# Moving a clip, a store and half a weight transfer in a Mamba2 block with a gated feed-forward

## The chip, the cores and the metric

The kernel runs on one core of one Trainium2 chip. A core has TensorE (PE in the profile, with its weight loads as PEld), VectorE (DVE), ScalarE (ACT), GpSimd (POOL) and SyncE (SP), which here only issues transfers. The metric is the time of one execution on the device, in microseconds, lower is better. Three executions of the kernel before took 349.08, 349.23 and 349.53 us; the median is 349.23 us.

## The reference

Two stages, one behind the other. The first is a Mamba2 state-space block over 4 batches, 8 heads, 768 positions, head dimension 32 and state dimension 16, in chunks of 32. The second is a feed-forward layer on the 3072 x 256 result: 2048 hidden columns with a quick GELU, and back to 256.

```python
log_a = np.log(np.clip(a, 1e-06, 1.0))
for c in range(nc):
    cum = np.cumsum(la, axis=-1)
    L = np.exp(cum[..., :, None] - cum[..., None, :]) * causal
    y_intra = einsum(CB * L, xc)
    y_inter = einsum(Cc, state) * np.exp(cum)
    y[:, :, sl] = y_intra + y_inter
    state = decay_full * state + sum(Bx)
...
h = x @ w_in
g = h * (1.0 / (1.0 + np.exp(-1.702 * h)))
return g @ w_out
```

The weights `w_in` and `w_out` come as float64, the decays `a` as float32.

## The kernel before

The 3072 tokens are worked through in six groups (g) of 512. The state-space block of a group is done in two pairs (p) of 256 tokens, so pair 2 and pair 3 belong to group 1. While the feed-forward of one group runs on TensorE, the state-space work of the next is put between its matmuls. The order of every engine's instructions is the order of the program: `in_order` ties each instruction to the one before it on its engine. So an instruction that waits holds up all that stands behind it on that engine.

**The weights.** Both weight matrices arrive as pairs of 32-bit words and are turned into float32 on the chip, in ten pieces. Pieces 0 to 3 are two blocks of `w_in` each (128 hidden columns a block), pieces 4 and 5 four blocks each, pieces 6 to 9 four blocks of `w_out` each. For piece i:
- `fetch(i)` (line 163) issues two transfers on SyncE (line 180), one per half k of the 256 input rows. Pieces 0 and 1 share one buffer. With `held`, an engine first writes one element of the buffer (line 171), so that a transfer which overwrites this element has to wait for that engine to get there.
- `fields(i)` (lines 192 and 195) takes exponent and mantissa apart on VectorE, into `p` (power) and `m`.
- `clamp(i)` (lines 203 and 204) limits the exponent on ScalarE, in two instructions.
- `rounded(i)` (line 208) adds the low word on VectorE.
- `join(i, parts)` (lines 222 and 228) puts sign, exponent and mantissa together on VectorE and writes `w_in` or `w_out`; with parts = 2 in two rounds, so that the first blocks are ready sooner. It needs `clamp(i)`. After join(1) follows fetch(6), after join(5) fetch(9).
- `narrow(i)` (line 235) is rounded(i), fields(i + 1) and join(i), with the join ahead of the fields for pieces 4 and 5, there in two parts.

**The first group.** At the start SyncE issues B, piece 0 and the four transfers of x for pairs 0 and 1. Then comes `fetch(1, held=nc.gpsimd)`: GpSimd writes element 0 of the buffer after its first `since_start`, and SyncE's transfers of pieces 1 to 5 and of `az` (the decays) follow. After that TensorE computes the hidden blocks f = 0 to 15 of group 0 (`hidden`, matmuls L895, activations L898). What is put behind each of them stands in `in_hidden[0]`: narrow(2) after block 1, narrow(3) after 2, narrow(4) after 4, narrow(5) after 8, narrow(6) after 11, narrow(7) after 14, and clamp(3) to clamp(8) after blocks 1, 2, 7, 11, 14 and 15. Work that is put behind the same block runs in the order in which it was added.

**The decays.** `az` holds `a` for the six chunks of 128 of each row. `clip(t, name)` (lines 356 to 361) limits its values, copies the first column of every half chunk into `starts` and sets these columns to zero in `az`. `store_a` (line 1225) clips all of `az` and has SyncE store it into `scratch` in DRAM (two transfers, line 1228); it runs after block 5, ahead of fetch(7), fetch(8) and the load of pair 3. `pick_a` (line 369) makes X from chunks 4 and 5 of `az` on ScalarE after block 8. `fan_all` after block 9 spreads X over the partitions with TensorE (ab, line 415, and the rows of lines 504 and 533) and scans it on VectorE (`decay_heads`, line 453); `since_fanned` (lines 543 to 546) follows. These serve pair 2. For pair 3, `spread` (line 259) reads `scratch` back into the tile `a`, and `spread_rows(1)` (line 268) reads `af`; both are issued after block 9.

**The projection of group 0** (`project_all`, matmuls L992 into o) has its own list, `in_project[0]`: the transposes of pair 2, rounded(8), fields(9) and join(8) at step 0; at step 2 `decay(3)` (scan at line 405 over `a`, then Be, line 464), `clip_rows(1)` and `decay_rows(1)` (lines 483 to 496, over `af`) and the transposes of pair 3, whose last part is `since_start(3)` (CsT, line 670). At step 9 TensorE takes `score` (cb, line 685) and `gain` (A, line 716).

```python
at(in_hidden[0], 5, store_a, lambda: fetch(7), lambda: fetch(8),
   lambda: load(PG + 1))
at(in_hidden[0], 8, lambda: pick_a(PG))
at(in_hidden[0], 9, lambda: fan_all(PG))
at(in_hidden[0], 9, since_fanned)
```

Of the kernel before, what the change touches and what calls it, by code (L numbers as in the profile page):

```python
# [8 lines left out]
FP32 = mybir.dt.float32  # L9
# [7 lines left out]
P = 128  # L17
# [18 lines left out]
def kernel(  # L36
# [31 lines left out]
    nc = tc.nc  # L68
# [6 lines left out]
    BH = NB * NH  # L75
# [7 lines left out]
    CG = TG // P  # L83
    NP = T // (2 * P)
    PG = CG // 2
# [9 lines left out]
    const = ctx.enter_context(tc.tile_pool(name="const", bufs=1))  # L95
# [10 lines left out]
    az = ffn.tile([P, 4 * TG // 2], FP32, tag="mg", name="az", bufs=3)[:, :NC * P].rearrange(  # L106
        "p (c s) -> p c s", c=NC)
# [8 lines left out]
    def load_blocks(p, queues=(nc.sync, nc.sync)):  # L116

        g, n = divmod(p, PG)
        b, c = divmod(2 * p, NC)
        for queue, name, src in zip(queues, "CB", (C, B)):  # L120
            if n == 0:
                blocks[name, g] = raw.tile([P, 2, PG * P], FP32, tag="z", name=f"z{name}{g}", bufs=2)
            for r in range(R):
                queue.dma_start(
                    out=blocks[name, g][32 * r:32 * r + 32, :, n * P:(n + 1) * P],
                    in_=src[b, Q * r:Q * r + Q, c * P:(c + 2) * P].rearrange(
                        "q (i f) n -> i q (f n)", i=32))
# [10 lines left out]
    def load(p, parts=None):  # L138
        if parts is None:
            parts = "bcx" if p < 2 * PG else "bx"  # L140
            if p >= 2 * PG:
                load_blocks(p)
        for part in parts:
            dst, src, e = {"b": (rb, B, N), "c": (rc, C, N), "x": (rx, x, D)}[part]
            dst[p] = raw.tile([P, 2, NH, e], FP32, tag=part, name=f"{part}{p}",
                              bufs=2 if part == "c" else 3)
            for k in range(2):
                b, c = divmod(2 * p + k, NC)
                sl = slice(c * P, (c + 1) * P)
                nc.sync.dma_start(out=dst[p][:, k], in_=src[b, :, sl, :].rearrange("h s d -> s h d"))  # L150
# [9 lines left out]
    def words(name):  # L160
        return wide.tile([P, 2 * PN], U32, tag="bits", name=name, bufs=BUFS)

    def fetch(i, held=False):
        name, f, n = PIECES[i]
        if n == 2 and f % 4:
            t = pieces.pop(i - 1)[:, 2 * n * DM:]
        else:
            t = pieces[i] = words(f"bits{i}")
            t = t[:, :2 * n * DM]
        if held:  # L170
            held.memset(t[:, :1], 0)
        if name == "in":
            src = moe_w_in[:, 2 * f * P:2 * (f + n) * P].rearrange("(k p) e -> p k e", p=P)
            dst, src = (v.rearrange(s, h=n, e=2 * P) for v, s in (
                (t, "p (h k e) -> k p h e"), (src, "p k (h e) -> k p h e")))
        else:
            src = moe_w_out[f * P:(f + n) * P, :].rearrange("(f p) (h e) -> h p f e", p=P, h=2)
            dst = t.rearrange("p (h f e) -> h p f e", h=2, f=n)
        for k in range(2):
            nc.sync.dma_start(out=dst[k], in_=src[k])  # L180
        t = t.rearrange("p (e w) -> p e w", w=2)
        bits[i] = t[:, :, 0], t[:, :, 1]
# [5 lines left out]
    def fields(i):  # L188
        hi, cols = bits[i][1], slice(0, PIECES[i][2] * DM)
        mantissa[i] = wide.tile([P, PN], U32, tag="m", name=f"m{i}")[:, cols]  # L190
        power[i] = wide.tile([P, PN], U32, tag="p2", name=f"p2{i}")[:, cols]
        nc.vector.tensor_scalar(out=power[i], in0=hi, scalar1=0x7FF00000, scalar2=None,
                                op0=ALU.bitwise_and)

        nc.vector.tensor_scalar(out=mantissa[i], in0=hi, scalar1=0x000FFFFF,
                                scalar2=0x00100000, op0=ALU.bitwise_and, op1=ALU.bitwise_or)
# [9 lines left out]
    def rounded(i):  # L206

        nc.vector.scalar_tensor_tensor(out=mantissa[i].bitcast(FP32), in0=bits[i][0],
                                       scalar=2.0 ** -32, in1=mantissa[i],
                                       op0=ALU.mult, op1=ALU.add)  # L210
# [4 lines left out]
    def join(i, parts=1):  # L215

        name, f, n = PIECES[i]
        n //= parts
        low, m, p2 = bits.pop(i)[1], mantissa.pop(i), power.pop(i)
        for k in range(parts):  # L220
            cols, fs = slice(k * n * DM, (k + 1) * n * DM), slice(f + k * n, f + (k + 1) * n)
            nc.vector.scalar_tensor_tensor(out=p2[:, cols], in0=low[:, cols], scalar=0x80000000,  # L222
                                           in1=p2[:, cols], op0=ALU.bitwise_and, op1=ALU.bitwise_or)
            if name == "in":
                dst, h = w_in[:, fs].rearrange("p f k e -> p (f k e)").unsqueeze(1), 1
            else:
                dst, h = w_out[:, :, fs].rearrange("p c f e -> p c (f e)"), 2
            nc.vector.scalar_tensor_tensor(  # L228
                out=dst, in0=m[:, cols].bitcast(FP32).rearrange("p (h e) -> p h e", h=h),
                scalar=2.0 ** -20, in1=p2[:, cols].bitcast(FP32).rearrange("p (h e) -> p h e", h=h),  # L230
                op0=ALU.mult, op1=ALU.mult)
        for n in NEXT.get(i, ()):
            fetch(n)

    def narrow(i):
        rounded(i)
        if i in (4, 5):
            join(i, 2)
        if i + 1 < len(PIECES):
            fields(i + 1)  # L240
        if i not in (4, 5):
            join(i)


    scratch = dram.tile([NC, 2, NB * NH, H], FP32, name="scratch")
# [106 lines left out]
    starts, fans, flat = {}, {}, {}  # L352

    def clip(t, name):

        nc.vector.tensor_scalar(out=t, in0=t, scalar1=1e-6, scalar2=1.0,
                                op0=ALU.max, op1=ALU.min)
        starts[name] = const.tile([P, t.shape[1], 2], FP32, name=f"starts{name}")
        first = t.rearrange(by_chunk, s=2)[:, :, :, 0]
        nc.vector.tensor_copy(starts[name], first)  # L360
        nc.vector.memset(first, 0.0)

    def pick_a(p):

        b, c = divmod(2 * p, NC)
        X = ffn.tile([P, 2, DM], FP32, tag="ob", name=f"X{p}")
        X = fans[p] = X.rearrange("p k (q i) -> p k q i", q=Q)
        for q in range(Q):
            nc.scalar.activation(X[:, :, q], az[:, c:c + 2], AF.Copy, scale=pick[:, b, q:q + 1])
# [13 lines left out]
    for i, n, head in ((0, 1, PG), (1, 2, PG), (0, 0, 1)):  # L383
        t = whose[32 * i:32 * i + 32, n:n + 1]
# [116 lines left out]
    def fan_rows(t, c0, c1, o):  # L501

        o = o[:, :(c1 - c0) * P]
        nc.tensor.matmul(out=o, lhsT=whose[:32, 0].rearrange("p h n -> p (h n)"),
                         rhs=t[:32, c0:c1].rearrange("p c s -> p (c s)"), start=True,
                         stop=True, tile_position=(0, 0), skip_group_check=True)
        return o
# [21 lines left out]
    def fan_since():  # L529
        o = bank("rows4")  # L530
        t = fanned["rows"] = fan_rows(az, CG, NC, o)
        f = fanned["starts"] = o[:, 2 * P:2 * P + 2 * (NC - CG)]
        nc.tensor.matmul(out=f, lhsT=whose[:32, 0].rearrange("p h n -> p (h n)"),
                         rhs=starts[1][:32, CG:].rearrange("p c s -> p (c s)"), start=True, stop=True,
                         tile_position=(0, 0), skip_group_check=True)

    fanned = {}
# [46 lines left out]
    def bank(name):  # L584
        return ps.tile([P, 4 * P], FP32, tag="ff", name=name)
# [634 lines left out]
    def at(places, i, *work):  # L1220
        places.setdefault(i, []).extend(work)

    in_hidden = [{} for _ in range(NG)]
    in_project = [{} for _ in range(NG)]
    def store_a():
        clip(az, 1)
        for i, side in enumerate(SIDES):
            nc.sync.dma_start(out=scratch[:, i].rearrange("c r i -> r c i"), in_=az[:32, :, side])

    at(in_hidden[0], 5, store_a, lambda: fetch(7), lambda: fetch(8),  # L1230
       lambda: load(PG + 1))
    at(in_hidden[0], 8, lambda: pick_a(PG))
    at(in_hidden[0], 9, lambda: fan_all(PG))
    at(in_hidden[0], 9, since_fanned)
    for i, k, c in ((2, 1, 1), (3, 2, 2), (4, 4, 7), (5, 8, 11), (6, 11, 14), (7, 14, 15)):
        at(in_hidden[0], k, lambda i=i: narrow(i))
        at(in_hidden[0], c, lambda i=i: clamp(i + 1))
    at(in_hidden[0], 9, lambda: spread(PG + 1), lambda: spread_rows(1))
    n, p = 2 * PG, 3 * PG
# [105 lines left out]
    for g in range(2, NG):  # L1345
        n, p = (g + 1) * PG, (g + 2) * PG
# [103 lines left out]
```

## Time and profile before

| | |
|---|---|
| median of three executions | 349.23 us (349.08 to 349.53) |
| the profiled execution, whole | 350.67 us |
| its span | 348.80 us |
| TensorE busy | 341.6 us (98%) |
| VectorE busy | 254.6 us (73%) |
| ScalarE busy | 155.0 us (44%) |
| GpSimd busy | 13.1 us (4%) |
| bytes moved | 25.92 MB |

A row of a timeline has the start in us from the beginning of the span, the duration in us, the engine (with q for its queue or sequencer, as in SPq), the line of the kernel, the operation, output<-inputs by the names of the tiles without their numbers, the shape, and how many instructions are merged in the row. In brackets stands how long the engine was idle before it, and what ended that. A float32 matmul appears as two records. A row of SyncE gives the time that issuing took; when the bytes land is told by the semaphore that the transfer raises.

### The profile page before, as it was taken

What the parts mean: (1) busy time and instruction counts of PE and PEld (TensorE: products, weight loads), DVE (VectorE), ACT (ScalarE), POOL (GpSimd) and SP (SyncE); (2) the same over time, 40 slices, a digit from 0 to 9 for tenths busy, and PEclk for the clock granted to TensorE, in tenths of its full rate; (3) what the DMA queues carried; (4) which work ended last, traced back from release to release, by engine and by line L of the source; (5) the groups of instructions that cost most, each with busy time, mean ns of one, the idle gap of its engine ahead of it and who ended that gap; (6) DMA issues with size and microseconds to landing.
All of it is one profiled execution on the core that took longest, in us unless ns stands there. A gap on an engine that the chain in (4) does not pass through costs nothing.

```text
span 348.8 us, 8124 instructions
## 1 busy us (share of the span) xinstructions
PE 341.6 (98%) x3380; PEld 268.9 (77%) x3380; DVE 254.6 (73%) x481; ACT 155.0 (44%) x352; POOL 13.1 (4%) x42
## 2 busy tenths in 40 slices
PE   8989999999999999999999999999999999999996
PEld 6634444445688888888888888888888888899996
DVE  5889997999878999667997467788465654465463
ACT  4797585205453322654432554332564331554320
POOL 8300000100000100000000000000000000000000
PEclk9999999999999999999999999999999999999999
DMA  6599889624627200415704027400000300000301
GB/s 158 134 300 213 189 181 245 113 54 105 113 49 131 66 0 2 75 57 124 123 18 63 0 59 130 73 1 2 0 4 3 55 7 0 0 2 0 62 0 61
DMA packets 89980, 25.92 MB, mean 74 GB/s; under 512 B 73432, under 2 KB 87128, under 8 KB 89944
## 3 DMA queue, kind: packets, MB, share of 16 engines
q1 hardware_dynamic: 89112, 24.88, 33.5%
q10 hardware_dynamic: 832, 0.52, 0.5%
q8 instruction: 26, 0.43, 0.5%
q14 instruction: 10, 0.08, 0.1%
HBM read 22.15 MB, written 3.24 MB: 73 GB/s over the span
## 4 chain that ended last, share of the span: by engine, by line
PE 90%; DMA 3%; DVE 2%; SPq 1%; ACT 1%; issue 1%; ACTq 1%; POOL 0%; DVEq 0%
PE acc L1055 28%; PE X L950 19%; PE Y L960 14%; PE o L992 8%; PE acc L1062 7%; PE h L895 5%; DMA bits<-in_moe_w_in_dram 3%; PE y L839 2%; PE cb L685 2%; PE y L825 1%; SPq L180 1%; PE A L716 1%; PE ab L557 1%; DMA zC<-in_C_dram 1%; DVE p L222 1%
## 5 line engine op out<-in xcount | busy, mean ns | idle before, releaser
L955 ACT ACTIVATE ac<-X 128x256 f32<-128x256 f32 x76 | 29.1, 383 | 81.5 <-PE X L950 80.7
L1082 DVE TENSOR_TENSOR gT<-Y,ac 128x512 f32<-128x512 f32 x38 | 26.2, 689 | 40.1 <-PE Y L960 32.5
L1055 PE MATMUL acc<-mg,mw 128*128 128x256 f32 x192 | 54.5, 379 | 0.0
L927 ACT ACTIVATE gT<-gT 128x512 f32<-128x512 f32 (+1 forms) x76 | 38.9, 518 | 29.0 <-DVE gT L1082 28.5
L950 PE MATMUL X<-my,mi 128*128 128x256 f32 x152 | 45.1, 380 | 0.0
L1055 PEld LDWEIGHTS acc<-mg,mw 128*128 128x128 f32 x192 | 36.5, 190 | 5.0
L895 PE MATMUL h<-yT,w_in 128*128 128x512 f32 x80 | 35.6, 598 | 1.1 <-DVE w_in L228 0.6
L1082 DVE TENSOR_TENSOR gT<-Y,b 128x256 f32<-128x256 f32 x38 | 15.9, 419 | 28.5 <-PE Y L960 28.5
L1055 PE MATMUL acc<-gT,w_out 128*128 128x256 f32 x128 | 35.5, 379 | 0.0
L950 PEld LDWEIGHTS X<-my,mi 128*128 128x128 f32 x152 | 28.0, 190 | 3.9 <-ACT ac L955 0.2
L895 PEld LDWEIGHTS h<-yT,w_in 128*128 128x128 f32 x80 | 14.7, 190 | 19.7 <-issue 15.9
L992 PE MATMUL o<-gT,w_out 128*128 128x512 f32 x64 | 28.3, 595 | 0.0
L918 DVE TENSOR_TENSOR mg<-gT 128x512 f32<-128x512 f32 x40 | 27.2, 681 | 0.0
L1055 PEld LDWEIGHTS acc<-gT,w_out 128*128 128x128 f32 x128 | 24.2, 190 | 3.4 <-ACT yT L873 0.2
L955 ACT ACTIVATE b<-X 128x256 f32<-128x256 f32 x38 | 14.6, 383 | 21.2 <-PE X L950 20.7
L950 PE MATMUL X<-yT,w_in 128*128 128x256 f32 x76 | 23.2, 389 | 0.0
L960 PE MATMUL Y<-yT,w_in 128*128 128x256 f32 x76 | 22.7, 381 | 0.0
L960 PE MATMUL Y<-my,mi 128*128 128x256 f32 x76 | 22.7, 380 | 0.0
L960 PE MATMUL Y<-yT,mi 128*128 128x256 f32 x76 | 22.5, 379 | 0.0
L950 PE MATMUL X<-my,w_in 128*128 128x256 f32 x76 | 22.5, 379 | 0.0
L992 PEld LDWEIGHTS o<-gT,w_out 128*128 128x128 f32 x64 | 11.8, 190 | 13.6 <-issue 13.4
L405 DVE TENSOR_TENSOR_SCAN L<-a,idents 128x1024 f32<-128x1024 f32 x9 | 20.5, 2277 | 0.2 <-DMA a<-scratch 0.2
(159 smaller groups left out, 546.9 us busy)
## 6 DMA issues: line engine op xcount, KB each, us to landing
a<-scratch SPq DMA_DIRECT2D x18, 256.0 KB, 4.8
bits<-in_moe_w_out_dram SPq DMA_DIRECT2D x8, 512.0 KB, 6.6
x<-in_x_dram SPq DMA_DIRECT2D x24, 128.0 KB, 3.1
out_dram<-ob SPq DMA_DIRECT2D x40, 64.0 KB, 1.9
bits<-in_moe_w_in_dram SPq DMA_DIRECT2D x8, 256.0 KB, 4.4
bits<-in_moe_w_in_dram SPq DMA_DIRECT2D x4, 512.0 KB, 11.9
b<-in_B_dram SPq DMA_DIRECT2D x20, 64.0 KB, 2.6
af<-in_a_dram SPq DMA_DIRECT2D x3, 384.0 KB
```

The costliest lines, as they stand in the source:

```text
L405: nc.vector.tensor_tensor_scan(out=L, data0=ra[p].rearrange("p k e -> p (k e)"), data1=idents.rearrange("p h i -> p (h i)"), initial=0.0, ...
L685: nc.tensor.matmul(out=s["cb"][side, r, k].rearrange("p (q i) -> p q i", q=Q), lhsT=BT[rows, k, side], rhs=CT[rows, k, :, side], start=Tru ...
L895: nc.tensor.matmul(out=h, lhsT=w_in[:, f, k], rhs=yT[g][:, k], start=(k == 0), stop=(k == NK - 1), skip_group_check=True)
L918: nc.vector.tensor_tensor(out=t[:, 0:2], in0=B[:, :, 1], in1=B[:, 0], op=ALU.subtract)
L927: nc.scalar.activation(o, i, AF.Silu, scale=GELU_SCALE)
L950: nc.tensor.matmul(out=s["X"], lhsT=lhsT, rhs=rhs, start=i == "1", stop=i == "4", skip_group_check=True)
L955: nc.scalar.activation(copy, s["X"], AF.Copy)
L960: nc.tensor.matmul(out=o, lhsT=lhsT, rhs=rhs, start=s.pop("new", False), stop=i != "5", skip_group_check=True)
L992: nc.tensor.matmul(out=o[c], lhsT=w_out[:, c, f], rhs=gT[g, f // 2][:, f % 2], start=(f == 0), stop=(f == NF - 1), skip_group_check=True)
L1055: nc.tensor.matmul(out=acc[g][0][i][:, cols], lhsT=w, rhs=h[:, cols], start=(j == 0 and k == 0 and (i, 0) in begins), stop=(j == NF // 2 - ...
L1062: nc.tensor.matmul(out=o[k] if type(o) is list else o[:, cols], lhsT=h[:, cols], rhs=w, start=(j == 0 and (i, k) in begins), stop=(j == NF ...
L1082: nc.vector.tensor_tensor(out=o, in0=v, in1=w, op=ALU.add)
```

## The change

- The element that GpSimd writes before piece 1 is no longer element 0 but element 256. The transfer of half k = 0 writes elements 0 to 255 and 512 to 767 of the piece, half k = 1 writes 256 to 511 and 768 to 1023. So only the second half overwrites the element.
- narrow(2) has its join ahead of fields(3). narrow(3) has its join in two parts, still behind fields(4).
- The clip of `az` is split. Chunks 4 and 5 (all 128 partitions) are clipped inside narrow(4), between join(4) and fields(5), and leave the starts that `fan_since` uses. Chunks 0 to 3 (32 partitions) are clipped in `store_a`, without starts.
- `store_a` stands after block 9, behind since_fanned and ahead of the spread of pair 3, not after block 5.
- `pick_a` stands after block 7, ahead of clamp(5), not after block 8.

```diff
         if held:
-            held.memset(t[:, :1], 0)
+            held.memset(t[:, 2 * P:2 * P + 1], 0)
...
     def narrow(i):
         rounded(i)
-        if i in (4, 5):
-            join(i, 2)
+        if i in (2, 4, 5):
+            join(i, 1 if i == 2 else 2)
+        if i == 4:
+            clip(az[:, CG:], 1)
         if i + 1 < len(PIECES):
             fields(i + 1)
-        if i not in (4, 5):
-            join(i)
+        if i not in (2, 4, 5):
+            join(i, 2 if i == 3 else 1)
...
-        starts[name] = const.tile([P, t.shape[1], 2], FP32, name=f"starts{name}")
+        if name:
+            starts[name] = const.tile([P, t.shape[1], 2], FP32, name=f"starts{name}")
         first = t.rearrange(by_chunk, s=2)[:, :, :, 0]
-        nc.vector.tensor_copy(starts[name], first)
+        if name:
+            nc.vector.tensor_copy(starts[name], first)
...
-                         rhs=starts[1][:32, CG:].rearrange("p c s -> p (c s)"), start=True, stop=True,
+                         rhs=starts[1][:32].rearrange("p c s -> p (c s)"), start=True, stop=True,
...
     def store_a():
-        clip(az, 1)
+        clip(az[:BH, :CG], 0)
...
-    at(in_hidden[0], 5, store_a, lambda: fetch(7), lambda: fetch(8),
-       lambda: load(PG + 1))
-    at(in_hidden[0], 8, lambda: pick_a(PG))
+    at(in_hidden[0], 5, lambda: fetch(7), lambda: fetch(8), lambda: load(PG + 1))
+    at(in_hidden[0], 7, lambda: pick_a(PG))
     at(in_hidden[0], 9, lambda: fan_all(PG))
-    at(in_hidden[0], 9, since_fanned)
+    at(in_hidden[0], 9, since_fanned, store_a)
```

## The prediction

> **What bounds the kernel now.** I read the page first, then the chain of waits up to 120 us, then the timeline of each engine from 11 to 69 us, and last when single transfers land.
>
> ```profile
> PE 341.6 (98%) x3380; PEld 268.9 (77%) x3380; DVE 254.6 (73%) x481; ACT 155.0 (44%) x352; POOL 13.1 (4%) x42
> ```
>
> TensorE is busy 98% of 348.8 us, so only holes in its work can be won, and any new hole is paid in full. The change touches work before 70 us, where the TensorE timeline has these holes:
>
> ```profile
> 18.38 7.18 PE L895 MATMUL h<-yT,w_in 128*128 128x512 f32 x16 [0.47 <-ACT yT L858]
> ...
> 26.18 10.57 PE L895 MATMUL h<-yT,w_in 128*128 128x512 f32 x24 [0.63 <-DVE w_in L228]
> ...
> 37.59 0.69 PE L415 MATMUL ab<-X,ones 32*64 32x256 f32 x16 [0.84 <-ACT X L369]
> ...
> 38.95 10.57 PE L895 MATMUL h<-yT,w_in 128*128 128x512 f32 x24
> ...
> 67.53 0.78 PE L716 MATMUL A<-x,Be 64*32 64x64 f32 x54 [0.31 <-DVE CsT L670]
> ```
>
> One block of the hidden layer is four records of 0.43, 1.72 us. Block 4 waits 0.63 for its weights; the 24 records after it take 10.57 where 24 x 0.43 = 10.3, so another 0.25 is lost (block 6); ab waits 0.84. The last line matters most: A waits for VectorE's CsT, so VectorE's chain at 67.5, and not TensorE, sets the rest. VectorE's own timeline:
>
> ```profile
> 22.50 0.69 DVE L208 SCALAR_TENSOR_TENSOR m<-bits,m 128x512 f32<-128x512 uint32 x1
> ...
> 23.94 0.43 DVE L192 TENSOR_SCALAR p<-bits 128x512 uint32<-128x512 uint32 x1 [0.75 <-DMA bits<-in_moe_w_in_dram]
> ...
> 26.87 0.69 DVE L192 TENSOR_SCALAR p<-bits 128x1024 uint32<-128x1024 uint32 x1 [0.24 <-DMA bits<-in_moe_w_in_dram]
> ...
> 34.41 0.55 DVE L356 TENSOR_SCALAR az<-az 128x768 f32<-128x768 f32 x1
> ...
> 36.35 0.70 DVE L222 SCALAR_TENSOR_TENSOR p<-bits,p 128x512 uint32<-128x512 uint32 x1
> ...
> 40.23 2.43 DVE L453 TENSOR_TENSOR_SCAN L<-ab,idents 128x256 f32<-128x256 f32 x4
> ...
> 57.72 0.69 DVE L192 TENSOR_SCALAR p<-bits 128x1024 uint32<-128x1024 uint32 x1 [1.77 <-DMA bits<-in_moe_w_out_dram]
> ...
> 61.32 2.28 DVE L405 TENSOR_TENSOR_SCAN L<-a,idents 128x1024 f32<-128x1024 f32 x1
> ...
> 64.05 0.56 DVE L483 TENSOR_SCALAR af<-af 128x768 f32<-128x768 f32 x1
> ...
> 67.04 0.42 DVE L670 TENSOR_TENSOR CsT<-tp,since 128x256 f32<-128x256 f32 x1
> ```
>
> It is full from 24 to 45 us, waits 1.77 for the last w_out piece, then runs without a break through decay(3) (61.32) to CsT. Its inputs a and af come through SyncE:
>
> ```profile
> 37.37 1.09 SPq L1228 DMA_DIRECT2D scratch<-az  x2
> 38.51 2.12 SPq L180 DMA_DIRECT2D bits<-in_moe_w_out_dram  x4
> ...
> 50.14 1.08 SPq L180 DMA_DIRECT2D bits<-in_moe_w_out_dram  x2
> 51.31 1.30 SPq L259 DMA_DIRECT2D a<-scratch  x2
> 52.66 0.72 SPq L268 DMA_DIRECT2D af<-in_a_dram  x1
> ```
>
> The store to scratch goes out 14 us before scratch is read back, and by its semaphore it has landed at 40.1. The pair a lands at 59.28 and 60.60, only 0.7 before decay(3) uses it, and af at about 63.2, 0.85 before 64.05.
>
> **The change part by part.**
>
> *First half of blocks 2 and 3 unheld.* SyncE issues the last x until 9.06, then waits 3.6 us for GpSimd's memset at 12.63. Now one transfer of 256 KB goes out at 9.1, behind x, and uses the stretch from 11 to 14 us in which the DMA engines are under 10% busy. All ten transfers behind the memset move up one issue (0.47 us). At 385 GB/s, the rate of 23 to 26 us, 256 KB less ahead is 0.68 us; at the 200 GB/s of 14 to 17 us, 1.3. Ends 0.5 and 1.3; I take 0.7, since the pieces land in the fast stretch. Pieces 3 and 4 landed at 23.85 and 26.75, now about 23.1 and 26.0. Cost: the last x landed at 11.92, and A (12.02) uses it in its last quarter, at 12.5; an x with 512 KB behind it (issued 49.21) took 3.85 us against 3.44, which gives 12.3: nothing, at most 0.4.
>
> *join(2) before fields(3).* It now waits for ScalarE's clamp(2), which ends at 23.64 by the row of before, not for a DMA: 23.68 to 25.09 instead of 24.62 to 26.03. TensorE's block 4 starts at 25.56, when block 3 ends: 0.63 gone. VectorE waits 0.45 instead of 0.75, and fields(4) starts at 26.48 instead of 26.87.
>
> *join(3) in halves.* Four instructions of 128x256 at the 0.40 spacing of 16.22 to 17.81 are 1.6 instead of 1.4: 0.2 more on VectorE, but block 6 has its weights at 28.6 and needs them at 29.0: 0.25 gone.
>
> *The clip split.* Narrow(4) ends at 33.13 (33.21 before). The half for chunks 4 and 5 is 128x256: 0.42 for 512 columns and 0.55 for 768 put it at 0.29, and the row of 0.50 for 128x256 at 4.28 is the upper end; with starts and memset 0.55 (0.45 to 0.8). It now stands before fields(5), where it stood behind it: fields(5) at 33.7 (33.21). X needs the clip: 33.8 to 34.7 on ScalarE, ahead of clamp(5), which takes 2.33 and ends at 37.0 (36.26). ab then never waits: TensorE gets there at 35.9 instead of 37.59, 1.7 us won. But join(5) waits for clamp(5): 37.05 instead of 36.35, and everything behind it on VectorE is 0.7 late. The other half (32x512, 0.42 by the row of that width, and memset) comes after since_fanned: another 0.5, less the 0.33 that fields(7) waited for a piece that now lands earlier. join(6) ends at 50.0 instead of 49.12. TensorE, finished with block 15 at 47.6, waits for these w_out blocks: o starts at 50.25 instead of 49.79. So the 1.7 won is given back at 50 us, and 0.45 more. At A this is 0.45 late against a wait of 0.3 to 0.48: nothing to speak of.
>
> *The store behind since_fanned.* On SyncE its two issues (1.14 us) no longer stand ahead of fetch(7), fetch(8) and the loads of pair 3; with the 0.7 above, fetch(9) goes out 1.1 to 1.9 earlier (48.6) and lands at 56.1 (55.5 to 56.4) instead of 57.59. VectorE is ready for it at 56.7, so decay(3) could start at 60.3, 1.0 earlier. But the store is now issued right behind fetch(9), at about 49.8, with 1 MB ahead of it in its queue (before, it landed 0.4 behind the x ahead of it), and the read of scratch right behind the store. The trace of before never shows this wait. I have SyncE hold the read until the store has landed. The Trainium skill, "DMA: Bandwidth & Descriptors", section "Two DMAs through the same engine are not ordered", says a dependent DMA must be issued only after the first one's completion semaphore; no run here shows what happens without it.
>
> The store lands at 56.1 (55.5 to 56.8). From there the pair a: unqueued pairs landed 5.3 us (76.51) and 5.5 (103.71) after the first issue; the pair with af behind it, as here, 6.55:
>
> ```profile
> 152.06 1.24 SPq L259 DMA_DIRECT2D a<-scratch  x2
> 153.40 0.64 SPq L268 DMA_DIRECT2D af<-in_a_dram  x1
> ```
>
> Nearest is the last; I take 6.0: a at 62.1 (60.8 to 63.3). af, 8.8 after the first issue there, is at 64.9, in time for a clip_rows at 64.9. decay(3) starts at 62.1 instead of 61.32, so CsT and A are 0.8 later. SyncE's later loads slip about 1 us, and the nearest user (79.33; landed by 74.1) has 5 to spare.
>
> **Sum.** TensorE: -0.63 -0.25 -0.84, given back at o, +0.45, absorbed at A; then +0.8 at A by the wait for a. The profiled execution, 350.67 (span 348.80 and 1.87 around it; 1.44 above the median), becomes 351.5; the median of 349.23 becomes 350.0.
>
> **Rivals.**
> 1. *The round trip is hidden.* If a lands by 61.3, A is bound by TensorE: -0.05, up to 0.2 either way; 349.2. For it: fetch(9) may go out 2 us earlier and two of three pairs took 5.4. Against it: the store has 1 MB ahead, and the pair that had af behind it took 6.55. The Trainium skill, "DMA: Bandwidth & Descriptors", section "Anatomy of one DMA", fits a fixed 2.0 us and 436 GB/s for transfers that GpSimd issues, by which (an estimate) the pair would land 3.2 us after its issue and be hidden; the trace, of SyncE's transfers, has 5.3 to 6.55.
> 2. *Faster: VectorE's chain is shorter than I count.* If ScalarE and the clip cost so little that join(6) ends by 49.0 and a lands by 60.5, A moves up with decay(3), at most 1.0: 348.4. For it: VectorE loses three DMA waits (0.75, 0.24, 0.33). Against: clamp(5) cannot start before power(5), which stands behind the clip. It decides when both are 0.7 earlier than my count.
> 3. *The half transfer is not free*, or stays held after all, because the memset lies between its columns: the queue gains nothing, a lands 0.7 later still, or A at 12 us slips 0.4: 350.8.
>
> **Numbers.** Forecast (a binds, 0.4 to 1.5 late) 0.47; rival 1 0.30; rival 2 0.15; rival 3 0.08. The bound for no change is 0.2%, 0.7 us, about what a measurement of this kernel can tell. Of the forecast's 0.47 some 0.06 lie under 0.7; rival 3 gives 0.07 to slower. So faster 0.17, same 0.35, slower 0.48. The range goes from rival 2's middle, 348.5, to 351.2, the pair at its slowest (+1.5 to +2); the forecast's own is 349.6 to 350.8.
>
> **What would show it.** Right: block 4 and ab without a hole; o's first matmul waiting for DVE w_out near 50; SyncE waiting for scratch; decay(3) waiting for DMA a near 62; A later than 68. Wrong: decay(3) starts without a DMA wait, or o waits for nothing at 48.2.

## The result and the profile after

The changed kernel took 353.52 us (median of six, 352.22 to 354.81), the kernel before, beside it, 349.15 us (median of six, 348.80 to 349.56). The ratio is 1.0124 with a 95% interval of 1.0101 to 1.0147: slower by 1.2%. The forecast was 350.0 and its range ended at 351.2, so the direction was right and the size was wrong. (The ratios leave out executions at a much lower clock, two of the kernel before at 503 us and one of e8 at 587 us, and are not always the quotient of the two medians.)

The profiled execution of the changed kernel took 352.22 us, the fastest of its six; its span is 350.2. The first part of its page:

```profile
PE 341.7 (98%) x3380; PEld 268.6 (77%) x3380; DVE 255.0 (73%) x485; ACT 155.0 (44%) x352; POOL 13.2 (4%) x42
```

TensorE does the same work; the time went into holes. Rows of its timeline from 11 to 69 us:

```profile
16.54 0.76 PE L843 MATMUL y<-L,x 64*32 64x64 f32 x53 [1.43 <-issue]
...
19.26 17.43 PE L899 MATMUL h<-yT,w_in 128*128 128x512 f32 x40 [0.47 <-ACT yT L862]
36.63 0.69 PE L419 MATMUL ab<-X,ones 32*64 32x256 f32 x16
...
50.59 3.67 PE L996 MATMUL o<-gT,w_out 128*128 128x512 f32 x8 [1.60 <-DVE w_out L228]
...
67.78 0.79 PE L720 MATMUL A<-x,Be 64*32 64x64 f32 x56
```

The hidden layer runs 40 records in 17.43 without a hole, and ab no longer waits: both as forecast. Then o waits 1.60 for VectorE's w_out, as forecast too, and A comes at 67.78 without a wait, which was not forecast. VectorE's timeline of the same kernel shows why o is late:

```profile
21.15 0.69 DVE L222 SCALAR_TENSOR_TENSOR p<-bits,p 128x512 uint32<-128x512 uint32 x1 [1.30 <-ACT p L204]
...
24.45 0.69 DVE L222 SCALAR_TENSOR_TENSOR p<-bits,p 128x512 uint32<-128x512 uint32 x1 [0.48 <-ACT p L204]
...
37.65 0.69 DVE L222 SCALAR_TENSOR_TENSOR p<-bits,p 128x512 uint32<-128x512 uint32 x1 [0.71 <-ACT p L204]
...
60.65 2.28 DVE L409 TENSOR_TENSOR_SCAN L<-a,idents 128x1024 f32<-128x1024 f32 x1
62.97 0.49 DVE L468 TENSOR_TENSOR Be<-b,L 128x128 f32<-128x128 f32 x2
63.74 0.56 DVE L487 TENSOR_SCALAR af<-af 128x768 f32<-128x768 f32 x1 [0.28 <-DMA af<-in_a_dram]
...
66.74 0.42 DVE L674 TENSOR_TENSOR CsT<-tp,since 128x256 f32<-128x256 f32 x1
```

VectorE waits for clamp(1) (1.30), clamp(2) (0.48) and clamp(5) (0.71), and for af by a little. decay(3) at 60.65 does not wait for a, which the prediction had named as a sign of being wrong. CsT is done at 67.16, 0.6 before A, so in this execution A is held by the late o and not by VectorE. SyncE's row of issues and its waits, in two answers:

```profile
46.42 1.08 SPq L180 DMA_DIRECT2D bits<-in_moe_w_out_dram  x2
47.59 1.24 SPq L1232 DMA_DIRECT2D scratch<-az  x2
53.01 1.35 SPq L261 DMA_DIRECT2D a<-scratch  x2
```

```profile
SPq L261 <- DMA scratch<-az: 4.1, 1, 4.1
```

SyncE stands 4.1 us at the read of scratch (total, times, longest). By the semaphores fetch(9) landed at 52.75, the store at 52.96 and 53.17, and the pair a at 58.99.

**The kernel before, a second time.** The prediction read an execution of 350.67 us. Among the other 81 timed executions of the kernel before (348.44 to 351.22), taken beside the result and the experiments, one was slower than that. So the same kernel was profiled once more, as e5: 349.15 us, span 347.2. Its TensorE timeline:

```profile
15.57 0.76 PE L839 MATMUL y<-L,x 64*32 64x64 f32 x53 [0.60 <-issue]
...
18.30 17.43 PE L895 MATMUL h<-yT,w_in 128*128 128x512 f32 x40 [0.47 <-ACT yT L858]
36.48 0.69 PE L415 MATMUL ab<-X,ones 32*64 32x256 f32 x16 [0.75 <-ACT X L369]
...
48.69 3.60 PE L992 MATMUL o<-gT,w_out 128*128 128x512 f32 x8
...
65.81 0.79 PE L716 MATMUL A<-x,Be 64*32 64x64 f32 x56
```

and its VectorE timeline:

```profile
20.19 0.69 DVE L222 SCALAR_TENSOR_TENSOR p<-bits,p 128x512 uint32<-128x512 uint32 x1 [0.45 <-ACT p L204]
...
58.38 2.29 DVE L405 TENSOR_TENSOR_SCAN L<-a,idents 128x1024 f32<-128x1024 f32 x1
...
64.10 0.42 DVE L670 TENSOR_TENSOR CsT<-tp,since 128x256 f32<-128x256 f32 x1
```

The hole at block 4, that at block 6 and the wait at A are not there. VectorE waits for no piece of weights, decay(3) starts 2.9 earlier than in the profile that the prediction read, and CsT is done at 64.5, 1.3 before A. Against this execution the changed kernel's TensorE is 0.96 late at y, 0.14 at ab (the 0.75 there is won), 1.90 at o, 1.97 at A, 2.5 at 113 us and 2.94 at 121 us, where X waits 0.35 for ac. That is the 3.0 between the spans.

The 0.96 at y is a part of this that no experiment ties to the change. It does not stay on TensorE: ScalarE's yT and the clamp(1) behind it come 0.96 later too, and so does VectorE's join(1) (21.15 against 20.19). So it is also in the 1.90 at o. Without it o is 0.94 late, and the same 0.94 is left in the two further profiles of e1 and e4 below (1.28 late at o with 0.34 at y, 1.42 with 0.48).

### The profile page after: what moved, and what is told of

The parts are those of the page before. It is cut to its first block, busy times and chain, and to the rows that moved or that the text cites. A ratio compares the mean times of both kernels' runs of the same rounds, so it can differ in the third digit from the quotient of the medians.

```text
span 350.2 us, 8134 instructions
## 1 busy us (share of the span) xinstructions
PE 341.7 (98%) x3380; PEld 268.6 (77%) x3380; DVE 255.0 (73%) x485; ACT 155.0 (44%) x352; POOL 13.2 (4%) x42
## 4 chain that ended last, share of the span: by engine, by line
PE 87%; DMA 4%; DVE 3%; SPq 3%; ACT 1%; issue 1%; POOL 0%; DVEq 0%
PE acc L1059 28%; PE X L954 19%; PE Y L964 14%; PE o L996 8%; PE acc L1066 7%; DMA bits<-in_moe_w_in_dram 3%; PE y L843 2%; PE h L899 2%; PE cb L689 2%; SPq L180 1%; PE y L829 1%; SPq L150 1%; PE A L720 1%; PE busy L447 1%; DMA c<-in_C_dram 1%
```

## The experiments

Four theories were set against each other. *Chain*: VectorE's clamp waits, the early clip and the late clip make w_out and o late. *Round trip*: the store behind fetch(9) makes a, af and so A late. *Queue*: the unheld half transfer disturbs x or the loads behind it. *Supply*: what delays TensorE is the hole ahead of y, which the profile puts down to "issue", because the new transfer is in flight when TensorE's next instructions are fetched.

**e1 and e4: the changed kernel with the half held again, and once more as it is.**

```diff
-            held.memset(t[:, 2 * P:2 * P + 1], 0)
+            held.memset(t[:, :1], 0)
```

> The changed kernel with the hold put back (the memset writes element 0 again), all else as changed. Theory S (instruction supply: the transfer that is no longer held keeps the DMA engines busy while TensorE's next 16 KB of instructions are fetched, and TensorE stands still): the loss goes with the hold; TensorE's idle time ahead of y (line 839 of before) is back at about 0.6 us and none stands ahead of A at 12 us, the first hidden matmul starts at 18.4, and the time is 348.6 to 349.4. Theory D (the loss is VectorE's: the clip ahead of fields(5) and the second half of the clip make join(6) late, and o waits for w_out): the time stays above 351.

> The changed kernel once more, for a second profile, since its first profiled execution is with 352.2 us the fastest of its six. Theory S: an execution of 353 to 355 has 2 to 4 us of issue gaps of TensorE before 20 us, where the first had 1.88. Theory D: the gaps ahead of 20 us are as in the first profile, and the rest stands at o or behind it.

e1 took 354.62 us (352.80 to 357.04), ratio 1.0173 (1.0140 to 1.0205); e4, which is the changed kernel unaltered, 353.01 (351.79 to 356.75), 1.0136 (1.0094 to 1.0177). Two rows of e1's TensorE, two of its VectorE, and two of e4's TensorE:

```profile
49.97 3.67 PE L996 MATMUL o<-gT,w_out 128*128 128x512 f32 x8 [1.60 <-DVE w_out L228]
...
69.21 0.78 PE L720 MATMUL A<-x,Be 64*32 64x64 f32 x54 [1.75 <-DVE CsT L674]
```

```profile
61.74 2.29 DVE L409 TENSOR_TENSOR_SCAN L<-a,idents 128x1024 f32<-128x1024 f32 x1 [1.62 <-DMA a<-scratch]
...
65.73 0.56 DVE L487 TENSOR_SCALAR af<-af 128x768 f32<-128x768 f32 x1 [1.17 <-DMA af<-in_a_dram]
```

```profile
50.11 3.67 PE L996 MATMUL o<-gT,w_out 128*128 128x512 f32 x8 [1.61 <-DVE w_out L228]
...
67.30 1.03 PE L720 MATMUL A<-x,Be 64*32 64x64 f32 x56
```

With the half held, both of VectorE's loads of pair 3 are late and A waits 1.75. The store landed at 55.59 (53.38 in e4), the second transfer of a at 61.65, 6.2 after SyncE issued the pair. So the unheld half does not harm the changed kernel, and the time stays above 351, as was put down for a loss on VectorE. Whether the half helps is less sure. The median with the half held is 1.1 to 1.6 higher, but the intervals of e1 and e4 overlap. The store landed 2.2 later in e1, but two profiles of one kernel can lie further apart than that: fetch(9) goes out at 50.14 in the first profile of before and at 46.30 in e5, at 45.8 to 49.7 in the seven profiles with the half unheld and at 46.3 to 50.1 in the eight with it held.

**e2 and e3: the half alone, and a foreign transfer in its place.** e2 is the kernel before with only the memset moved, as in the change. e3 leaves the memset where it was and adds a useless transfer of 256 KB behind the last x (its target in w_out is overwritten later):

```diff
     load(1, "x")
+    nc.sync.dma_start(out=w_out[:, 0, 0:4]..., in_=moe_w_in[:P, 8 * P:12 * P]...)
```

> The kernel before with nothing changed but the element that the memset writes (256 instead of 0), so the first half of blocks 2 and 3 is not held. Theory S: most of the loss is here: idle TensorE time of the kind issue ahead of A and y of 1.5 us or more in place of 0.58, time 351 to 354. Theory D: 348.6 to 349.4, a little faster if anything, as the pieces land 0.7 us earlier.

> The kernel before with one more transfer of 256 KB behind the last x (a part of w_in into a place of w_out that is overwritten later); every piece of the weights is held as before. It is work that is of no use. Theory S: the transfer alone does the harm, 350 to 354, with the issue gaps ahead of A or y larger than 0.58 together. If the harm came from the order of the pieces or from what is made of them earlier, and not from bytes in flight at 9 to 14 us: 349.2 to 349.9 (nothing, or the 0.7 us that 256 KB more cost the queue).

e2 took 349.09, ratio 1.0009 (0.9998 to 1.0020); e3 349.44, 1.0015 (1.0004 to 1.0025). e2's o starts at 48.69 and its A at 65.82, as in e5, and its hole at y is 1.01, e3's 0.73. Queue falls. Supply falls as the main cause: e2 has the new transfer and the hole of 1.01, yet its y starts at 15.58, as in e5 (15.57), because the matmuls ahead of the hole ended earlier; and with the half held again (e1) nothing is won. What remains of it is the 0.96 at y in the one execution above.

**e5: the kernel before, profiled once more.** No edit; it is shown above.

> The kernel before, unchanged, for a second profile. The first one was taken of an execution of 350.67 us, above all 29 others that were timed (348.44 to 349.64). Theory W (that execution was untypical: its weights came late, and the VectorE waits of 0.75, 0.24, 0.33 and 1.77 us for them are its own): this profile has a span near 347.2, none of these four waits over 0.3, no TensorE hole ahead of block 4 and none ahead of A, and w_out's first blocks 1.0 us or more before TensorE is ready for them at o. Theory F (the first profile was typical): the four waits come again, and A waits for CsT.

**e6: the changed kernel with the store back behind block 5.**

```diff
-    at(in_hidden[0], 5, lambda: fetch(7), lambda: fetch(8), lambda: load(PG + 1))
+    at(in_hidden[0], 5, store_a, lambda: fetch(7), lambda: fetch(8), lambda: load(PG + 1))
-    at(in_hidden[0], 9, since_fanned, store_a)
+    at(in_hidden[0], 9, since_fanned)
```

> The changed kernel with the store to scratch and the clip of chunks 0 to 3 put back behind block 5, all else as changed. Theory V (VectorE's chain: the sum of the moved clip, the wait for clamp and the halves makes w_out late for o, 1.3 us, and the store's round trip adds what A waits): the round trip goes, the half clip (0.44) falls into VectorE's wait for clamp(5), o's wait falls from 1.60 to 1.1 or 1.2, A waits for nothing, 350.4 to 351.8. Theory O (the loss at o alone, A's wait of 1.75 in one profile being chance): 352.4 to 353.2, only the 0.45 at o less.

350.96 us (350.09 to 352.18), ratio 1.0053 (1.0034 to 1.0071). Its TensorE:

```profile
48.99 3.67 PE L996 MATMUL o<-gT,w_out 128*128 128x512 f32 x8 [1.23 <-ACT gT L902]
...
66.18 0.79 PE L720 MATMUL A<-x,Be 64*32 64x64 f32 x56
```

This is within the 350.4 to 351.8 put down for round trip and chain together. More than half of the loss goes with the store's place (353.0 to 353.5 against 351.0), and o still waits 1.23. The row names ScalarE's gT, but the w_out that o needs is done at 48.85, 0.14 before o, the distance that it has in the changed kernel too (50.45 and 50.59), so this is VectorE's chain again. The half clip moves with the store, and o waits 0.37 less than in the changed kernel; so this run does not tell how much of the difference is the round trip alone.

**e9: the store's place alone, in the kernel before.** Chunks 4 and 5 are clipped where all of `az` was, chunks 0 to 3 and the store go behind since_fanned:

```diff
-    at(in_hidden[0], 5, store_a, lambda: fetch(7), lambda: fetch(8),
+    at(in_hidden[0], 5, lambda: clip(az[:, CG:], 1), lambda: fetch(7), lambda: fetch(8),
        lambda: load(PG + 1))
...
-    at(in_hidden[0], 9, since_fanned)
+    at(in_hidden[0], 9, since_fanned, store_a)
```

> The kernel before with the clip in two halves (chunks 4 and 5 where the whole clip stood, behind block 5) and the rest of the clip with the store behind since_fanned: the store's move alone. Theory R (round trip: the store lands behind fetch(9), only then is scratch read, a lands about 6 and af about 10 us after the store): the store lands near 53, a near 59 and af near 63 where VectorE could use them at 58.4 and 61.1; CsT comes 1 to 2.5 us late, of which A has 1.3 to 1.7 to spare: A waits 0 to 1.2, 349.2 to 350.8. If the round trip cost nothing: 348.8 to 349.3.

352.86 us (352.20 to 353.81), ratio 1.0101 (1.0078 to 1.0124). The profiled execution took 353.36. Its TensorE, its VectorE and its SyncE's longest wait:

```profile
48.45 3.60 PE L994 MATMUL o<-gT,w_out 128*128 128x512 f32 x8
...
68.16 1.11 PE L718 MATMUL A<-x,Be 64*32 64x64 f32 x54 [2.29 <-DVE CsT L672]
```

```profile
60.59 2.29 DVE L407 TENSOR_TENSOR_SCAN L<-a,idents 128x1024 f32<-128x1024 f32 x1 [2.38 <-DMA a<-scratch]
...
64.68 0.56 DVE L485 TENSOR_SCALAR af<-af 128x768 f32<-128x768 f32 x1 [1.26 <-DMA af<-in_a_dram]
```

```profile
SPq L259 <- DMA scratch<-az: 4.5, 1, 4.5
```

This is the round trip of the prediction, link by link: fetch(9) lands at 54.09, the store at 54.45, the pair is issued at 54.33 and lands at 60.50 (6.2 later), decay(3) waits for it, clip_rows waits for af, A waits for CsT. The size was missed once more: 349.2 to 350.8 and a wait of 0 to 1.2 at A had been put down, with the store landing near 53 and af near 63. And the time is more than the wait. A is 2.34 later than in e5 (68.16 against 65.82), and soon after it the same matmul of o is 3.72 later (71.64 against 67.92). The windows of this execution (stretch in us, its length, then busy time and instructions of PE, PEld, DVE, ACT and POOL, the granted clock, the DMA share and GB/s) say where the other 1.4 is:

```profile
66.00:68.00 2.00, 0.00 (x0) 0.00 (x0) 1.87 (x2) 0.00 (x0) 0.40 (x1) 0.98 0.17 44
68.00:70.00 2.00, 1.84 (x55) 1.36 (x56) 2.00 (x3) 0.67 (x4) 0.34 (x1) 0.50 0.79 82
70.00:72.00 2.00, 2.00 (x4) 0.86 (x3) 1.85 (x4) 1.03 (x6) 0.00 (x0) 0.66 0.83 137
72.00:74.00 2.00, 2.00 (x6) 0.95 (x5) 1.89 (x6) 0.00 (x0) 0.00 (x0) 1.00 0.21 56
```

The granted clock falls to 0.50 near the end of the wait and stays there for some 3.4 us (from 67.95 to 71.4), and a record takes 0.85 instead of 0.43. TensorE is busy in that stretch, so no list of holes shows it. Two of e9's four executions had a mean clock of 1.000 and still took 352.20 and 352.35, so most of the loss is there without it.

**e7 and e8: the other two parts alone, in the kernel before.** e7 has only the changed order of narrow:

```diff
-        if i in (4, 5):
-            join(i, 2)
+        if i in (2, 4, 5):
+            join(i, 1 if i == 2 else 2)
...
-            join(i)
+            join(i, 2 if i == 3 else 1)
```

e8 has only the early clip of chunks 4 and 5 in narrow(4) and pick_a after block 7; the other chunks and the store stay behind block 5.

```diff
+        if i == 4:
+            clip(az[:, CG:], 1)
...
-        clip(az, 1)
+        clip(az[:BH, :CG], 0)
...
-    at(in_hidden[0], 8, lambda: pick_a(PG))
+    at(in_hidden[0], 7, lambda: pick_a(PG))
```

> The kernel before with the order of narrow(2) and the halves of join(3) alone. Theory V: VectorE waits about 0.5 for clamp(2) and takes 0.2 more for the halves, 0.7 to 0.9 late at w_out, which is less than the 1.1 us that w_out has to spare at o in the profile of the kernel with the hold alone undone: 348.6 to 349.5. If every delay of VectorE's chain were paid in full: 349.7 to 349.9.

> The kernel before with the split clip (chunks 4 and 5 between join(4) and fields(5)) and pick_a behind block 7 alone; the rest of the clip and the store stay behind block 5. Theory V: the hole of 0.75 to 0.84 ahead of ab goes; fields(5) starts 0.6 later and join(5) waits 0.7 to 0.9 for clamp(5), w_out is 1.0 to 1.5 late, and o waits 0.6 to 1.2 in place of the hole: 348.5 to 349.8. If ab's hole were won whole: 348.2.

e7 took 349.88 (349.30 to 352.63), ratio 1.0039 (1.0016 to 1.0063); e8 350.07, ratio 1.0027 (1.0010 to 1.0044). One row of e7's TensorE, and one each of e8's VectorE and TensorE:

```profile
37.50 0.69 PE L415 MATMUL ab<-X,ones 32*64 32x256 f32 x16 [1.64 <-ACT X L369]
```

```profile
36.09 0.69 DVE L222 SCALAR_TENSOR_TENSOR p<-bits,p 128x512 uint32<-128x512 uint32 x1 [0.60 <-ACT p L204]
```

```profile
48.62 3.67 PE L996 MATMUL o<-gT,w_out 128*128 128x512 f32 x8 [0.49 <-DVE w_out L228]
```

In e7 the 0.48 of waiting for clamp(2) and the 0.2 of the halves push the clip back, and ab's hole grows from 0.75 to 1.64; the time is the one put down for the case that every delay of VectorE's chain is paid in full. In e8 ab's hole is gone, and 0.49 of it comes back at o; its 350.07 lies above the 349.8 put down. Both are small losses of their own. Together, e7 (+0.39%), e8 (+0.27%) and e9 (+1.01%) make 1.67%; e1, which has just these three parts, has 1.73%. With intervals of plus or minus 0.2 to 0.3% each this agrees, but it does not show that the parts add up; e13 below speaks against it.

**e10: the changed kernel with the store issued by GpSimd.**

```diff
-            nc.sync.dma_start(out=scratch[:, i].rearrange("c r i -> r c i"), in_=az[:32, :, side])
+            nc.gpsimd.dma_start(out=scratch[:, i].rearrange("c r i -> r c i"), in_=az[:32, :, side])
```

> The changed kernel, but the store to scratch is issued by GpSimd, not by SyncE; clip, order and place are those of the change. It no longer stands behind fetch(9) in SyncE's queue, so it lands soon after the clip (47 to 50 us), and SyncE reads scratch directly behind fetch(9). Theory R: A waits for nothing, o still waits 1.6: 350.6 to 352.0. Theory O (the loss is what o waits and what follows, and the round trip is hidden behind it): 352.6 to 353.6, as the changed kernel.

352.51 us (351.86 to 354.93), ratio 1.0074 (1.0053 to 1.0096). The store left at 45.09 and landed at 48.91 and 49.16, instead of behind fetch(9); A has no wait left. The time lies between the two ranges put down (350.6 to 352.0 and 352.6 to 353.6), so the store's wait in SyncE's queue is a part of the loss and not all of it. The profiled execution is the slowest of the six, 354.93, because w_out came late. Its TensorE, two rows of its VectorE, and two of its windows:

```profile
50.69 6.70 PE L996 MATMUL o<-gT,w_out 128*128 128x512 f32 x8 [2.79 <-DVE w_out L228]
```

```profile
45.83 1.10 DVE L192 TENSOR_SCALAR p<-bits 128x1024 uint32<-128x1024 uint32 x1
46.85 1.30 DVE L195 TENSOR_SCALAR m<-bits 128x1024 uint32<-128x1024 uint32 x1
```

```profile
52.00:54.00 2.00, 2.00 (x3) 0.68 (x3) 2.00 (x3) 1.65 (x2) 0.00 (x0) 0.50 1.00 319
54.00:56.00 2.00, 2.00 (x4) 0.73 (x3) 1.56 (x3) 1.65 (x4) 0.00 (x0) 0.50 1.01 273
```

The two rows of VectorE take 0.69 each in the changed kernel; here they cost w_out 1.0 more, beside GpSimd's store and a memset of GpSimd behind it (45.09 to 47.60). Whether GpSimd slows them was not tested. Eight records of o that take 3.67 elsewhere take 6.70: the clock is 0.50 from 50.0 to 56.8, twice as long as in e9, with a wait of 2.79.

**e13: the changed kernel with the old order of narrow.** The edit of e7, undone in the changed kernel.

> The changed kernel with the order of narrow of before (join(2) behind fields(3), join(3) in one part); clip, store, pick_a and the unheld half as changed. Theory of VectorE's chain: the 0.48 of waiting for clamp(2) and the 0.2 for halves are gone, w_out is ready near 49.1 instead of 49.8, o waits about 0.9 instead of 1.6, the store still lands behind fetch(9) and A does not wait or waits briefly; about 352.5, 0.5 to 1 us under the changed kernel. Rival: the weight pieces, not the order of narrow, set the chain, so that VectorE waits for a transfer what it no longer waits for clamp(2); then 353.3 as the changed kernel, with o still waiting 1.6.

353.02 us (351.29 to 355.35), ratio 1.0119 (1.0073 to 1.0165): no gain that can be told from the changed kernel. The median lies between the two values put down and does not decide between them: two of the four executions, with a mean clock of 1.000 or 0.999, took 351.29 and 351.70, the other two, with 0.995, 354.35 and 355.35. The profiled one took 351.70. Its TensorE and its VectorE:

```profile
49.45 3.67 PE L996 MATMUL o<-gT,w_out 128*128 128x512 f32 x8 [0.92 <-DVE w_out L228]
...
67.82 0.78 PE L720 MATMUL A<-x,Be 64*32 64x64 f32 x54 [0.88 <-DVE CsT L674]
```

```profile
64.34 0.56 DVE L487 TENSOR_SCALAR af<-af 128x768 f32<-128x768 f32 x1 [1.82 <-DMA af<-in_a_dram]
```

Chain gave the right wait at o (0.9 expected, 0.92 found). But what TensorE wins at o it waits out at A, now for af alone: against e4, whose y is as late (16.05 and 16.07), o is 0.66 earlier and A is not. The round trip sets a floor for A in each execution: CsT is done at 67.16 to 69.15 in the five profiles with the late store on SyncE (the changed kernel, e1, e4, e9, e13) and at 64.52 in e5. In the changed kernel A shows no wait only because o was later still; with o as early as in e5 it would, by CsT's row, have stood until about 67.2.

**e11 and e12: pick_a early, without the rest.** The experiments leave one part of the idea that is worth something: X made as soon as ScalarE has done clamp(5). e11 does only that in the kernel before; e12 adds the unheld half.

```diff
-    at(in_hidden[0], 8, lambda: pick_a(PG))
...
+        if i == 4:
+            at(in_hidden[0], c, lambda: pick_a(PG))
```

> The kernel before with X made directly behind clamp(5), ahead of block 8's activation, and nothing else: an attempt at a kernel faster than both. The clip has ended at 34.0 and clamp(5) at 35.15 in the second profile of before, so X ends 0.48 earlier and the hole of 0.75 ahead of ab falls to 0.3; VectorE's chain is untouched and w_out has 1.1 to spare at o. 348.4 to 348.7, if the 0.45 is not given back at A.

> The kernel before with two single parts put together: pick_a directly behind clamp(5), and the held element moved so that the first half of piece 1 goes out early. The theory of VectorE's chain: TensorE's hole ahead of ab shrinks from 0.75 to about 0.27, the unheld half adds nothing, o and A do not wait; of the 0.48 some 0.27 are given back at 118 us, where X waits for ac because the second load of a lands late; 348.6 to 348.9, ratio 0.998 to 1.000. If the unheld half is worth 1 us here, as it was in the changed kernel, then 347.8 to 348.1, ratio 0.996.

e11 took 348.68, ratio 0.9988 (0.9976 to 1.0001); e12 348.96, ratio 1.0002 (0.9978 to 1.0026). Two rows of e11's TensorE:

```profile
35.76 0.69 PE L415 MATMUL ab<-X,ones 32*64 32x256 f32 x16 [0.27 <-ACT X L369]
...
117.89 0.70 PE L950 MATMUL X<-my,mi 128*128 128x256 f32 x2 [0.27 <-ACT ac L955]
```

ab's hole goes from 0.75 to 0.27, and more than half of that is given back at 118 us. There the next pair's decay (VectorE's scan at line 405) waits 0.65 for its second load of a, against 0.31 in e5, and the work behind it on VectorE comes too late for X. e12 has the same 0.27 ahead of ab and no hole at 118; its profiled span is 346.7, e11's 346.8, e5's 347.2. Neither kernel is shown to be faster than the one before, and the unheld half adds nothing here.

## Why the prediction was wrong

**Its base.** The sum ended at 351.5 for "the profiled execution" and was then lowered by the 1.44 by which that execution stood above the median. This is the step that failed: it took the 1.44 for a constant that lies around the work. It lay ahead of A, in the very stretch that the change touches. The first matmul of o behind A starts at 68.23 in the execution the prediction read and at 66.53 in e5 (66.54 in e2), 1.70 apart, where the spans are 1.6 apart. So the holes credited at block 4 (0.63), at block 6 (0.25) and at A (0.31), and VectorE's four waits for weights, were that execution's own, and the median had no such holes to lose. Put against e5, the same forecast of that matmul (68.23 + 0.8 = 69.03) is 2.5 late, and 349.15 + 2.5 makes 351.65, close to the fastest executions of the changed kernel (351.79 and 352.22) and outside the range given. That is 1.65 of the 3.5 between forecast and result; the rest is in the store's price below and in what stays open.

**Unheld half.** "x nothing, at most 0.4": right, e2 is at 1.0009. The 0.7 (0.5 to 1.3) by which the queue was to come forward can't be checked at the store, where profiles with and without the hold overlap (fetch(9) at 45.8 to 49.7 and 46.3 to 50.1). One profile, e13, has a wait of 0.24 for x at 12.85, which was allowed for.

**join(2) first and the halves.** The wait for clamp(2) was put at 0.45 and is 0.48; the halves cost the 0.2 foreseen. But they were to take the place of a wait of 0.75 for a transfer and to close two holes. In e5 there is no such wait and no such hole, so both are plain cost: e7.

**The clip.** ab without a wait, o waiting for w_out "near 50", all as put down. That o at 50.25 was forecast and 50.59 measured is partly luck, since 0.96 of the 50.59 came from y (49.97 in e1, 50.11 in e4). The early clip takes 0.61 (0.55 forecast), the late one 0.44 (0.5). What was wrong is again what it was compared with: o at 48.69 in e5, not at 49.79, and no wait at A to absorb the rest.

**The store.** The chain SyncE, a, decay(3), CsT, A exists, and e9 shows it alone. But in the changed kernel a was not what bound: decay(3) waits for it neither in the first profile nor in e4 and e13, but only in e1 (1.62). fetch(9) was put at 56.1 and landed at 52.75, or 55.24 with the half held (e1). The pair lands 6.0 to 6.2 after its issue, as taken. af was put at 8.8 after the first issue; the first VectorE instruction on it starts 10.2 to 10.7 after it (65.73 - 55.47 in e1, 64.68 - 54.33 in e9, 63.74 - 53.01 in the changed kernel), and in e13 af alone holds A. So "in time" was wrong for af, by 1.4 to 1.9. The price at A was put at 0.8, since decay(3) stood at 61.32; against e5, where it stands at 58.38, A is 2.3 late in e9, 2.0 in e13 and 3.4 in e1, the last two with late work ahead of A in them.

**The rivals.** Rival 1, the round trip hidden, looks true in the profile of the changed kernel, where A has no wait; e13 shows that it is hidden only behind another loss, the late o. Rivals 2 and 3 fell: nothing was faster, and the half transfer did no harm that the times show.

**Not in the prediction.** First, the granted clock at a long wait, 1.4 in e9 and about 3 in e10, and the hole ahead of y. Second, 0.26 to 0.36 at 118 to 124 us, where X waits for ac. It is in every kernel with the changed store's place and also in e6 and e11, and not in e5, e2, e3, e7, e8 and e12. It goes with a longer wait of VectorE for loads at 107 to 113 us: 0.65 to 0.94 in the eight profiles that have it, 0.32 or less in the seven that don't. What decides that was not settled.

**What stays open.** The profile accounts for 352.22, 1.3 under the median. No execution of the changed kernel at its median was profiled. One of its six had a mean granted clock of 0.994; a stretch of 3.4 us at half clock would lower the mean over 350 us to 0.995, and the executions of e1, e4, e7, e9 and e13 at 0.994 or 0.995 are the longest of each (355.41 to 357.04 against 352.80 to 353.83 in e1). That the same stretch stands in them is argued from the clock's mean, not shown. It cannot explain the median of the changed kernel: four of the six took 353.43 to 353.63 with a mean clock of 0.999 or 1.000. Where the 1.3 of these executions lies is open.

## What to carry to other kernels

Before a sum is made against a profiled execution, see where its time stands among the timed ones; where it lies above nearly all of them, its waits may be its own, and a forecast is safer as the new start of the work that binds, compared with a typical execution, than as holes taken away. A store that is read back through a busy queue cost the landing of all that was issued ahead of it and a round trip behind it (here 6 us for a, 10 to 11 until af could be used), so it is issued early; from another queue (e10) A's wait was gone too. When two late inputs meet at one instruction, taking away the one that shows a wait only uncovers the other.

## What the runs showed of the hardware that was not expected

**A wait can halve the clock.** In e9 TensorE waited 2.29 and in e10 2.79. In both the granted clock fell to 0.50 about 2.1 us into the wait (at 67.9 after 65.9, at 50.0 after 47.9) and stayed there for 3.4 and 6.8 us. With waits of 1.60 (changed kernel), 1.61 (e4) and 1.75 (e1), in the profiled executions, it stayed at 1.00. The Trainium skill, "TensorE: Matmul & The Clock Gate", section "Part 1: The HAM clock gate (the "warmup" mystery)", says the clock is gated to a half or open, by free-running windows of about 3.4 us. The two values and the durations of one and two such windows agree with the traces. The Trainium skill gives there an idle window of about 3.4 us as what closes the gate; here a wait of 2.29 was enough. Two of e9's four executions had a mean clock of 1.000; how long TensorE waited in them is not known. Nor is it known for the one of e12's twelve executions that took 353.57 with a mean clock of 0.990; in the profiled one no wait of TensorE behind 20 us is over 0.3.

**A small store lands with what stands ahead of it.** Behind the 1 MB of fetch(9) in SyncE's queue the store landed 0.2 to 0.4 after fetch(9) (52.96 and 53.17 after 52.75 in the changed kernel; 54.27 and 54.45 after 54.09 in e9). The first of its two transfers took 5.2 to 6.0 from issue to landing in e1, e4, e9, e13 and the changed kernel, and 3.8 when GpSimd issued it (e10).

**A hole that no wait of the program explains.** Ahead of y, after 75 of 128 matmuls of one form, TensorE stood 0.28 to 1.43 with "issue" as the only cause, differently in every profile. In all fifteen profiles the hole ends 1.2 to 1.5 after the end of a 16 KB transfer of the kind "instruction" (12.92 + 1.26 and 15.65 in the first profile of before, 14.17 + 0.97 and 16.54 in the changed kernel). That TensorE waits there for its instructions is argued from this, not shown. y starts at 15.14 to 16.54, so a single execution moves by up to 1 us, and no experiment here tied it to the change.
